# Attention's first pair and third load put in another order, and the first weight sums of the last expert layer ahead of the last mixes of the chunk before it

## The chip, the cores and the metric

The kernel runs on one NeuronCore of a Trainium2 chip. The metric is the device time of one execution in microseconds (us). Beside it stands the span of a profiled execution, from its first to its last instruction. TensorE (PE in the profile, PEld its weight loads) multiplies and transposes, VectorE (DVE), ScalarE (ACT) and GpSimd (POOL) work elementwise, and SyncE (SP) issues most of the transfers.

## The reference

Two parts, in float32. Part one is attention with rotary embedding for 2 batches of 8 heads, 576 tokens and head size 64; its output, 1152 tokens by 512, goes into part two, a dense mixture of 4 experts.

```
q_rot, k_rot = rotate(q), rotate(k)          # [x1*cos - x2*sin, x1*sin + x2*cos]
scores = scale * q_rot @ k_rot^T
attn = exp(scores - max) / sum
x = (attn @ v), heads side by side           # 1152 x 512
p = probs / sum(probs)
out = sum over e of p[:, e] * (relu(x @ w1[e]) @ w2[e])   # 512 -> 1024 -> 512
```

## The kernel before

Every float32 operand of a product is split into a high part in fp32r and a low part (value minus high part), and a product is the sum of three fp32r matmuls. ScalarE makes a high part (`wh`, `sh`, `hH`), GpSimd or VectorE the low one (`wl`, `sl`, `hL`).

**Attention** takes the heads in pairs: pairs 0 to 3 of batch 0 (list `first`), which run alone, and four of batch 1 (list `second`), which run beside the experts of chunk 0. A pair loads `rawk`, `rawq`, `rawv` (`Pair.load`), rotates k and q (`Pair.rotate`: two products into `t1` and `t2`, a sum, a split into `hlk` and `hlq`), transposes them on TensorE into a PSUM tile (`tpk`, `tpq`, the last 64 tokens `tlk`, `tlq`, `tlkq`) and copies that out with ScalarE (`kT`, `qT`). `k2T` is `kT` with its halves swapped, made by two transfers of `Pair.swap`. Then nine units u follow: scores `sc`, maximum `mx` on VectorE, exponential `e` on ScalarE, transposes `pp` and `x` of it, split `ptH`, `ptL`, `ptX`, and values. Pair 0 is rotated in pieces: tokens of head 0 and the tails first (columns 0 to NS), head 1 (columns NS to NC, four tiles of 64, 256 elements a partition) after. The score tiles and the `tpk`, `tpq` of a head share two PSUM buffers (tag `s`), used in turn. Pairs 0, 2 use the buffers `evens`, pairs 1, 3 `odds`, so pair 2's load writes the buffers from which pair 0 was rotated.

The order is written out by hand: `Agenda.at(t, f)` puts a step at a time t in units, and `run` calls the steps in the order of t; the times are tables (`FIRST_TURNS`, `TURNS`, `ALONE`). An engine executes what it was given in that order. A step of `load_qk(t, pr)` loads k and q of a pair and queues its rotation on GpSimd, of which `work` issues a piece every half unit.

**Experts.** Chunk 0 is 512 tokens, chunk 1 is 640. `Weights` loads w1 and w2 in blocks of 512 KB (`wr`, named chunk, expert, matrix, block) into `NRAW` = 2 raw buffers, and splits them into `wh` and `wl` (rings of 5). A raw block's buffer comes free when its last reader is done, which is GpSimd's `wl`, or VectorE for a block that is only summed. For chunk 0, `Moe.expert` makes the hidden layer and then four outputs `po`, which `mix` adds into `acc` on VectorE and, for the last expert, stores.

**The seam** is the passage from chunk 0 to chunk 1. For chunk 1 the first layer runs as seven products of half size in place of eight (`Moe1.product`, p1 to p7). They need sums of weight blocks (`Weights.sum`: four VectorE operations into `sf`, then `sh`, `sl`) and sums of x (`Quarters`). For expert 0 of chunk 1, blocks of w1 are loaded twice, once for `wh`, `wl` (matrix 0) and once for the sums (matrix 2), and then w2 (matrix 1). The first layer computes p1 and p2 of all four blocks (i = 0 to 3), then for each block p6, p7, p5, p4, p3. Each product goes to the next of eight PSUM banks (`Moe1.bank`), ScalarE copies p1 out, VectorE adds (`p`, `u`, `v`), ScalarE makes `hH` and VectorE `hL`. The second layer's `po` take the next five banks.

Of the kernel before, what the change touches and what calls it, by code (L numbers as in the profile page):

```python
# [49 lines left out]
]  # L50
FIRST_TURNS = dict(q0=(1.327, 1.797), q1=(1.739, 1.84), q_tails=(-0.037, 0.16), swap=0.18)
NEXT_TURNS = dict(tails=(-0.01, -0.008), k=(0.03, 0.056), q=(0.975, 1.004))
# [3 lines left out]
def kernel(  # L56
# [402 lines left out]
    class Weights:  # L459
# [14 lines left out]
        def load(self):  # L474
            if self.loaded == len(self.order):
                return
            key = self.order[self.loaded]
            c, e, which, fb = key
            lo, hi = fb * FB * P, (fb + 1) * FB * P
            src, f = (w2[e, lo:hi, :], DM) if which == 1 else (w1[e, :, lo:hi], FB * P)  # L480
            raw = wpool.tile([P, FB * DM], F32, tag="raw", name="wr%d_%d_%d_%d" % key, bufs=NRAW)
            nc.sync.dma_start(
                out=raw.rearrange("p (a f) -> p a f", f=f), in_=src.rearrange("(a p) f -> p a f", p=P)
            )
            self.raw[key] = raw, f
            self.loaded += 1
# [33 lines left out]
        def next(self):  # L520
            self.load()
            self.split()

    class Moe:
# [3 lines left out]
        def __init__(self, ctx, c, n_ps, lead):  # L528
            self.c = c
            self.lead, self.ph = lead, {}  # L530
            self.n = ctok[c]
# [11 lines left out]
        def expert(self, e):  # L543
# [24 lines left out]
            for f in range(NF):  # L568
                fb, fi = divmod(f, FB)
                wH, wL = (w[:, fi, :] for w in wts.got[c, e, 1, fb])  # L570
                for t in range(n // P):
# [4 lines left out]
                    if f == NF - 1:  # L576
                        self.mix(e, t, po[t])
                if e == E - 1 and f == NF - 2:
# [115 lines left out]
    class Moe1(Moe):  # L694
# [7 lines left out]
        def __init__(self, ctx, quarters):  # L702
# [6 lines left out]
            ]  # L709
            self.used = 0  # L710
            self.x, self.lows = {}, []

        def bank(self, name):
            x = self.pp.tile([P, 512], F32, tag=f"m{self.used % 8}", name=name)
            self.used += 1
            return x

# [56 lines left out]
        def first_layer(self, e):  # L774
# [3 lines left out]
            if e == 0:  # L778
                wts.split()
                wts.next()  # L780
                for p in ("p1", "p2"):
                    for i in range(nb):
                        self.product(e, i, p)
                wts.next()
            for i in range(nb):
                for p in ("p6", "p7", "p5", "p4", "p3") if e == 0 else ("p1", "p6", "p7", "p5", "p2", "p4", "p3"):
                    self.product(e, i, p)
                    if p == "p4":
                        wts.next()
                if e == 0 and i < 2:  # L790
                    wts.next()
# [147 lines left out]
    pr.keep_tails("k", True)  # L939
    pr.split_v(nc.scalar)  # L940
    nx.rotate_now("k", nc.gpsimd)
    nx.rotate_now("q", nc.gpsimd)
    nx.split_v()
    pr.rotate_now("k", nc.vector, NS, NC)
    rest = pr.rotate("q", nc.vector, NS, NC)
    for _ in range(3):
        next(rest)
    plan.at(1.5, lambda: next(rest))
    pr.turn_heads("k", (1,))
    pr.keep_heads("k", (1,))  # L950
    turn(FIRST_TURNS["q0"], pr, "q", (0,), False, (2, NR))
# [20 lines left out]
    for hp, pr in enumerate(first):  # L972
# [3 lines left out]
        if hp + 1 < NP:  # L976
# [7 lines left out]
            plan.at(n + t["swap"], nx.swap)  # L984
    load_qk(7.2, first[2])
    load_v(U + 5.8, first[2])
# [11 lines left out]
    chunk0 = ExitStack()  # L998
    tpool, quarters = [], []

# [4 lines left out]
    def start_experts():  # L1005
        spare.close()
        tpool.append(ctx.enter_context(tc.tile_pool(name="tpool", bufs=1)))
        moe = Moe(chunk0, 0, 4, 0).steps()
        for i in range(E * 2 * NF):
# [42 lines left out]
    plan.run()  # L1052
    chunk0.close()
    attn.close()


    with ExitStack() as chunk1:
        moe = Moe1(chunk1, quarters[0])
        wts.pool = moe.h
        for e in range(E):  # L1060
            moe.expert(e)
# [43 lines left out]
```

## Time and profile before

| what | value |
|---|---|
| median of 3 runs | 588.01 us (587.08 to 590.39) |
| the profiled execution | 588.56 us |
| its span | 586.8 us |
| TensorE busy | 548.2 us (93% of the span) |
| VectorE, ScalarE, GpSimd busy | 341.3, 279.4, 331.0 us |
| the chain that ended last | TensorE 73%, VectorE 11%, ScalarE 6%, GpSimd 5%, transfers 2%, issue 2% |
| mean granted TensorE clock | 0.990 |

TensorE's busy time is the largest, and the difference to the span, 38.6 us, is where it stood idle. The chain that ended last is followed back from the last instruction to whatever released each step; where it leaves TensorE, another engine or a transfer decided. The granted clock is the share of full speed that TensorE was given in a stretch: 1.00 is 2.4 GHz, 0.50 is 1.2 GHz. All times below count from the start of the span.

### The profile page before, as it was taken

Reading aid. Unit: us, or ns where it says so; the run is one execution under the profiler, and the core shown is the slowest. Engines: PE = TensorE matmul, PEld = TensorE weight load, DVE = VectorE, ACT = ScalarE, POOL = GpSimd, SP = SyncE. Lnnn points to the kernel's source line nnn. Section 1 sums busy time; section 2 is a strip of 40 time slices with the busy share of each in tenths; the row PEclk is TensorE's granted clock in tenths of the full one; section 3 lists DMA queues with packets and bytes.
Section 4 is the critical chain, followed back from the end, with each engine's and each line's share of the span. In section 5 each row is a group of like instructions: output and inputs, shape, how many; then the busy total and the mean of one; then the engine's idle time right before and its main releaser. Section 6 shows DMA issues by size and latency. Waiting matters only on the chain.

```text
span 586.8 us, 8596 instructions
## 1 busy us (share of the span) xinstructions
PE 548.2 (93%) x3229; PEld 480.3 (82%) x3229; DVE 341.3 (58%) x596; ACT 279.4 (48%) x545; POOL 331.0 (56%) x222
## 2 busy tenths in 40 slices
PE   3788888899999999999999998898999999999996
PEld 2677778788888888888888886896899889889985
DVE  6786889524353443444334435777678677767702
ACT  4685797456443555455436553444244335323400
POOL 6949991366933694279335386366663683465300
PEclk9998999899999999999999999899999999999999
DMA  5053232055125312532232222433233124223002
GB/s 152 18 158 78 63 99 60 0 150 175 45 73 156 92 37 72 135 113 73 72 100 77 67 73 71 144 110 106 74 107 108 47 81 126 68 74 104 8 0 89
DMA packets 42459, 50.67 MB, mean 86 GB/s; under 512 B 7218, under 2 KB 32050, under 8 KB 42418
## 3 DMA queue, kind: packets, MB, share of 16 engines
q1 hardware_dynamic: 41618, 49.38, 28.5%
q10 hardware_dynamic: 800, 0.75, 0.5%
q8 instruction: 25, 0.41, 0.3%
q14 instruction: 16, 0.13, 0.1%
HBM read 43.34 MB, written 2.36 MB: 78 GB/s over the span
## 4 chain that ended last, share of the span: by engine, by line
PE 73%; DVE 11%; ACT 6%; POOL 5%; DMA 2%; issue 2%; SPq 0%; ACTq 0%; DVEq 0%; POOLq 0%
PE po L808 6%; PE po L809 6%; PE po L810 6%; PE p L729 5%; PE p L730 5%; PE p L731 5%; PE sc L282 4%; PE ph L596 4%; PE ph L598 4%; PE ph L597 4%; PE po L575 4%; PE po L573 4%; PE po L574 4%; PE pp L315 3%; PE x L417 2%; ACT e L301 2%
## 5 line engine op out<-in xcount | busy, mean ns | idle before, releaser
L142 POOL TENSOR_TENSOR wl<-wr,wh 128x1024 fp32r<-128x1024 f32 x64 | 155.2, 2427 | 131.3 <-ACT wh L135 131.3
L135 ACT ACTIVATE wh<-wr 128x1024 fp32r<-128x1024 f32 x64 | 67.4, 1053 | 39.6 <-PE po L575 16.6
L293 DVE TENSOR_REDUCE mx<-sc 128x1 f32<-128x576 f32 x72 | 54.0, 752 | 35.8 <-PE sc L282 35.2
L142 POOL TENSOR_TENSOR sl<-sf,sh 128x1024 fp32r<-128x1024 f32 x16 | 38.6, 2417 | 50.2 <-ACT sh L135 46.2
L301 ACT ACTIVATE e<-sc,mx 128x576 f32<-128x576 f32 x72 | 53.3, 740 | 27.4 <-DVE mx L293 26.8
L808 PE MATMUL po<-wh,hH 128*128 128x512 f32 x160 | 62.6, 391 | 2.6 <-DVE hL L769 2.6
L809 PE MATMUL po<-wl,hH 128*128 128x512 f32 x160 | 62.3, 389 | 0.0
L810 PE MATMUL po<-wh,hL 128*128 128x512 f32 x160 | 62.3, 389 | 0.0
L559 DVE SCALAR_TENSOR_TENSOR hL<-ph,hH 128x512 fp32r<-128x512 f32 x32 | 22.1, 691 | 61.0 <-ACT hH L558 61.0
L315 PE MATMUL pp<-ident,e 128*128 128x128 f32 x288 | 45.7, 283 | 7.2 <-DVE e L387 4.2
L573 PE MATMUL po<-wh,hH 128*128 128x512 f32 x128 | 52.3, 409 | 0.0
L596 PE MATMUL ph<-xH,wh 128*128 128x512 f32 x128 | 51.5, 402 | 0.0
L332 ACT ACTIVATE ptH<-pp 128x512 fp32r<-128x512 f32 x64 | 38.1, 595 | 25.6 <-PE x L365 17.2
L575 PE MATMUL po<-wh,hL 128*128 128x512 f32 x128 | 50.2, 392 | 0.0
L598 PE MATMUL ph<-xH,wl 128*128 128x512 f32 x128 | 50.1, 392 | 0.0
L574 PE MATMUL po<-wl,hH 128*128 128x512 f32 x128 | 50.0, 391 | 0.0
L597 PE MATMUL ph<-xL,wh 128*128 128x512 f32 x128 | 50.0, 391 | 0.0
L336 DVE TENSOR_TENSOR ptL<-pp,ptH 128x512 fp32r<-128x512 f32 x64 | 43.8, 685 | 10.1 <-ACT ptH L332 9.6
L513 DVE TENSOR_TENSOR sf<-wr 128x256 f32<-128x256 f32 x32 | 39.3, 1268 | 15.5 <-DMA wr<-in_moe_w_dram 15.4
L767 ACT ACTIVATE hH<-p 128x320 fp32r<-128x320 f32 x64 | 27.4, 434 | 43.3 <-DVE p L759 43.0
L315 PEld LDWEIGHTS pp<-ident,e 128*128 128x128 f32 x288 | 34.6, 144 | 14.2 <-issue 4.1
L135 ACT ACTIVATE sh<-sf 128x1024 fp32r<-128x1024 f32 x16 | 17.0, 1060 | 59.1 <-DVE sf L513 59.1
(163 smaller groups left out, 1380.6 us busy)
## 6 DMA issues: line engine op xcount, KB each, us to landing
wr<-in_moe_w_dram SPq DMA_DIRECT2D x68, 512.0 KB, 3.6
k2T<-kT SPq DMA_DIRECT2D x14, 288.0 KB, 4.1
rawv<-in_v_dram SPq DMA_DIRECT2D x8, 256.0 KB, 2.8
out_dram<-acc SPq DMA_DIRECT2D x8, 256.0 KB, 2.5
rawk<-in_k_dram SPq DMA_DIRECT2D x7, 256.0 KB, 4.2
rawq<-in_q_dram SPq DMA_DIRECT2D x7, 256.0 KB, 3.2
rawv<-in_v_dram SPq DMA_DIRECT2D x16, 32.0 KB, 2.5
tabs<-in_rope_dram ACTq DMA_DIRECT2D x1, 320.0 KB, 3.4
```

Of the source, the lines that this page charges most:

```text
L135: nc.scalar.activation(out=hi, in_=src, func=AF.Copy)
L142: eng_l.tensor_tensor(out=lo, in0=src, in1=f32(hi), op=ALU.subtract)
L315: nc.tensor.transpose(pp[:, c * P : (c + 1) * P], self.e[u][:, c * P : (c + 1) * P], ident)
L573: nc.tensor.matmul(po[t], lhsT=sH, rhs=wH, start=(f == 0), stop=False)
L574: nc.tensor.matmul(po[t], lhsT=sH, rhs=wL, start=False, stop=False)
L575: nc.tensor.matmul(po[t], lhsT=sL, rhs=wH, start=False, stop=(f == NF - 1))
L596: nc.tensor.matmul(o, lhsT=wH[:, kt], rhs=xh, start=(kt == 0), stop=False)
L597: nc.tensor.matmul(o, lhsT=wH[:, kt], rhs=xl, start=False, stop=False)
L598: nc.tensor.matmul(o, lhsT=wL[:, kt], rhs=xh, start=False, stop=(kt == KT1 - 1))
L808: nc.tensor.matmul(po[t], lhsT=sH, rhs=wH, start=(f == 0), stop=False)
L809: nc.tensor.matmul(po[t], lhsT=sH, rhs=wL, start=False, stop=False)
L810: nc.tensor.matmul(po[t], lhsT=sL, rhs=wH, start=False, stop=(f == NF - 1))
```

## The change

Three edits.

1. **First pair.** The rotation of q of head 1 goes from VectorE to GpSimd, ahead of the rotations of pair 1. The transposes of k of head 1 leave the shared score buffers for the bank `xb[1]` and move behind the scores of unit 1; the copies of q move (`FIRST_TURNS`), and the swap of head 1 to unit 1.4.
2. **Third load.** k and q of pair 2 (`first[2]`) are loaded at unit 2.6 instead of 7.2.
3. **Seam.** The four mixes of chunk 0's last expert are kept back (`mixes`); ahead of them stand two loads and the sums of block 0, behind them a load and the sums of block 1. p1 goes to banks m4 to m7 and p2 to m0 to m3. Blocks 2 and 3 of matrix 2 get raw buffers of their own in a pool `sums`. The splits in `first_layer` of expert 0 move on by about half a block.

```diff
-FIRST_TURNS = dict(q0=(1.327, 1.797), q1=(1.739, 1.84), q_tails=(-0.037, 0.16), swap=0.18)
+FIRST_TURNS = dict(q0=(1.327, 1.45), q1=(2.3, 2.5), q_tails=(-0.037, 0.16), swap=1.4)
...
-            raw = wpool.tile([P, FB * DM], F32, tag="raw", name="wr%d_%d_%d_%d" % key, bufs=NRAW)
+            late = which == 2 and fb >= NRAW
+            raw = (self.pool if late else wpool).tile(
+                [P, FB * DM], F32, tag="raw", name="wr%d_%d_%d_%d" % key, bufs=NRAW
+            )
...
-                        self.mix(e, t, po[t])
+                        self.mixes.append((e, t, po[t]))
+                        if e < E - 1:
+                            self.mix(*self.mixes.pop())
...
-            self.used = 0
+            self.used, self.ahead = 4, [self.bank(f"p2_{i}", i) for i in range(4)]
...
-        def bank(self, name):
-            x = self.pp.tile([P, 512], F32, tag=f"m{self.used % 8}", name=name)
-            self.used += 1
-            return x
+        def bank(self, name, i=None):
+
+            if i is None:
+                i, self.used = self.used, self.used + 1
+                if 8 <= i < 12:
+                    return self.ahead[i - 8]
+            return self.pp.tile([P, 512], F32, tag=f"m{i % 8}", name=name)
...
-                wts.split()
-                wts.next()
                 for p in ("p1", "p2"):
                     for i in range(nb):
                         self.product(e, i, p)
-                wts.next()
+                wts.split()
             for i in range(nb):
...
-                    if p == "p4":
+                    if p == "p4" and (e or i):
                         wts.next()
-                if e == 0 and i < 2:
+                if e == 0 and i == 0:
+                    wts.split()
+                elif e == 0 and i in (1, 2):
                     wts.next()
...
+    pr.rotate_now("q", nc.gpsimd, NS, NC, odds)
     nx.rotate_now("k", nc.gpsimd)
...
-    rest = pr.rotate("q", nc.vector, NS, NC)
-    for _ in range(3):
-        next(rest)
-    plan.at(1.5, lambda: next(rest))
-    pr.turn_heads("k", (1,))
-    pr.keep_heads("k", (1,))
+    plan.at(1.1, lambda pr=pr: pr.turn_heads("k", (1,), tp=xb[1].bitcast(F32R).unsqueeze(1)))
+    plan.at(1.3, lambda pr=pr: pr.keep_heads("k", (1,)))
...
-    load_qk(7.2, first[2])
+    load_qk(2.6, first[2])
...
+        wts.pool = chunk1.enter_context(tc.tile_pool(name="sums", bufs=1, side="right", reuse_waits="tile"))
+        wts.load()
+        wts.load()
+        wts.split()
+        for x in moe0[0].mixes:
+            moe0[0].mix(*x)
+        chunk0.close()
+        wts.load()
+        wts.split()
         moe = Moe1(chunk1, quarters[0])
-        wts.pool = moe.h
```

What this makes of the order of instructions is shown at three places. The first is TensorE in pair 0, from the scores of unit 0 on; before:

```order
L231 MATMUL tpk_0_238<-identr,hlk_00_149 128x128 x4
L282 MATMUL sc_0_0_245<-kT_0_185,qT_0_188 128x288 x2
L282 MATMUL sc_0_0_245<-k2T_0_197,qT_0_188 128x288 x2
L254 MATMUL tlq_00_250<-identr,hlq_00_158 128x128
L282 MATMUL sc_0_1_259<-kT_0_185,qT_0_188 128x288 x2
L282 MATMUL sc_0_1_259<-k2T_0_197,qT_0_188 128x288 x2
L231 MATMUL tpq_0_266<-identr,hlq_00_158 128x128 x2
L315 MATMUL pp_0_0_269<-ident,e_0_0_257 128x128 x4
L231 MATMUL tpq_0_281<-identr,hlq_00_158 128x128 x4
L282 MATMUL sc_0_2_287<-kT_0_185,qT_0_188 128x288 x2
```

After the change (`x_113` is the bank `xb[1]`):

```order
L282 MATMUL sc_0_0_241<-kT_0_185,qT_0_188 128x288 x2
L282 MATMUL sc_0_0_241<-k2T_0_197,qT_0_188 128x288 x2
L254 MATMUL tlq_00_246<-identr,hlq_00_158 128x128
L282 MATMUL sc_0_1_253<-kT_0_185,qT_0_188 128x288 x2
L282 MATMUL sc_0_1_253<-k2T_0_197,qT_0_188 128x288 x2
L231 MATMUL x_113<-identr,hlk_00_149 128x128 x4
L231 MATMUL tpq_0_265<-identr,hlq_00_158 128x128 x2
L315 MATMUL pp_0_0_268<-ident,e_0_0_251 128x128 x4
L282 MATMUL sc_0_2_281<-kT_0_185,qT_0_188 128x288 x2
L282 MATMUL sc_0_2_281<-k2T_0_197,qT_0_188 128x288 x2
L341 MATMUL x_112<-ident,e_0_0_251 64x128
L231 MATMUL tpq_0_291<-identr,hlq_00_158 128x128 x4
```

The four transposes of k of head 1 went from ahead of unit 0's scores to behind unit 1's, and those of q of head 1 from ahead of unit 2's scores to behind them.

The second is VectorE at the seam, from the first of the four mixes (`acc`) or of the sums (`sf`) on; before:

```order
L606 SCALAR_TENSOR_TENSOR acc_0_1511<-po_3_0_3673,probs,acc_0_1511 128x512
L606 SCALAR_TENSOR_TENSOR acc_1_1512<-po_3_1_3674,probs,acc_1_1512 128x512
L606 SCALAR_TENSOR_TENSOR acc_2_1513<-po_3_2_3675,probs,acc_2_1513 128x512
L606 SCALAR_TENSOR_TENSOR acc_3_1514<-po_3_3_3676,probs,acc_3_1514 128x512
L513 TENSOR_TENSOR sf_0_3979<-wr_0_2_0_3886 128x256 x2
L513 TENSOR_TENSOR sf_0_3979<-sf_0_3979,wr_0_2_0_3886 128x256
L513 TENSOR_TENSOR sf_0_3979<-wr_0_2_0_3886,sf_0_3979 128x256
L513 TENSOR_TENSOR sf_1_3990<-wr_0_2_1_3920 128x256 x2
```

After the change:

```order
L516 TENSOR_TENSOR sf_0_3964<-wr_0_2_0_3885 128x256 x2
L516 TENSOR_TENSOR sf_0_3964<-sf_0_3964,wr_0_2_0_3885 128x256
L516 TENSOR_TENSOR sf_0_3964<-wr_0_2_0_3885,sf_0_3964 128x256
L611 SCALAR_TENSOR_TENSOR acc_0_1510<-po_3_0_3672,probs,acc_0_1510 128x512
L611 SCALAR_TENSOR_TENSOR acc_1_1511<-po_3_1_3673,probs,acc_1_1511 128x512
L611 SCALAR_TENSOR_TENSOR acc_2_1512<-po_3_2_3674,probs,acc_2_1512 128x512
L611 SCALAR_TENSOR_TENSOR acc_3_1513<-po_3_3_3675,probs,acc_3_1513 128x512
L516 TENSOR_TENSOR sf_1_3985<-wr_0_2_1_3919 128x256 x2
```

The sums of block 0 went ahead of the mixes; those of block 1 stayed behind them.

The third is ScalarE in chunk 1's first layer, from the high part of the third sums (`sh_2`) on; before:

```order
L135 ACTIVATE sh_2_4089<-sf_2_4084 128x1024
L767 ACTIVATE hH_0_1_4120<-p_0_4112 128x320
L767 ACTIVATE hH_0_1_4120<-p_0_4124 128x320
L135 ACTIVATE sh_3_4141<-sf_3_4136 128x1024
L767 ACTIVATE hH_0_0_4042<-p_0_4145 128x320
L135 ACTIVATE wh_0_1_0_4157<-wr_0_1_0_4134 128x1024
L767 ACTIVATE hH_0_3_4188<-p_1_4180 128x320
L767 ACTIVATE hH_0_3_4188<-p_1_4192 128x320
L135 ACTIVATE wh_0_1_1_4204<-wr_0_1_1_4155 128x1024
```

After the change:

```order
L135 ACTIVATE sh_2_4093<-sf_2_4088 128x1024
L775 ACTIVATE hH_0_1_4124<-p_0_4116 128x320
L775 ACTIVATE hH_0_1_4124<-p_0_4128 128x320
L775 ACTIVATE hH_0_0_4051<-p_0_4138 128x320
L135 ACTIVATE sh_3_4153<-sf_3_4148 128x1024
L775 ACTIVATE hH_0_3_4184<-p_1_4176 128x320
L775 ACTIVATE hH_0_3_4184<-p_1_4188 128x320
L135 ACTIVATE wh_0_1_0_4200<-wr_0_1_0_3983 128x1024
L775 ACTIVATE hH_0_2_4061<-p_1_4204 128x320
L135 ACTIVATE wh_0_1_1_4216<-wr_0_1_1_4198 128x1024
```

`sh_3` moved behind the third `hH` of block 0, and `wh_0_1_0`, the first high part of w2, behind the two `hH_0_3` of block 1; each later split of w2 moved by as much.

## Rows read from the trace of the kernel before

**Rows 1.** Timeline, VectorE, first pair: start, length, engine, line, output<-inputs, shapes, count [idle before]
```profile
11.25 0.42 DVE L142 TENSOR_TENSOR hlk<-t1k,hlk 128x256 fp32r<-128x256 f32 x1
...
12.05 1.84 DVE L189 TENSOR_TENSOR t2q<-rawq,tabs 128x128 f32<-128x128 f32 x2
...
15.36 1.41 DVE L293 TENSOR_REDUCE mx<-sc 128x1 f32<-128x576 f32 x2
```

**Rows 2.** Timeline, ScalarE and TensorE, first pair
```profile
16.14 0.74 ACT L301 ACTIVATE e<-sc,mx 128x576 f32<-128x576 f32 x1 [2.09 <-DVE mx L293]
...
17.02 0.50 PE L231 MATMUL tpq<-identr,hlq 128*128 128x128 f32 x2 [2.23 <-ACT e L301]
...
24.40 0.30 PE L341 MATMUL x<-ident,e 128*64 128x128 f32 x1 [0.82 <-DVE ptX L348]
```

**Rows 3.** Timeline, GpSimd, first pair and start of the second
```profile
7.39 0.72 POOL L185 TENSOR_TENSOR t1q<-rawq,tabs 128x192 f32<-128x192 f32 x1
...
10.43 0.64 POOL L142 TENSOR_TENSOR hlq<-t1q,hlq 128x192 fp32r<-128x192 f32 x1
...
13.70 1.45 POOL L185 TENSOR_TENSOR t1k<-rawk,tabs 128x576 f32<-128x576 f32 x1
```

**Rows 4.** Timeline, GpSimd, rotation of pair 2
```profile
37.97 1.41 POOL L185 TENSOR_TENSOR t1k<-rawk,tabs 128x576 f32<-128x576 f32 x1 [8.23 <-DVE ptL L336]
...
43.44 1.40 POOL L142 TENSOR_TENSOR hlk<-t1k,hlk 128x576 fp32r<-128x576 f32 x1
...
50.15 1.42 POOL L142 TENSOR_TENSOR hlq<-t1q,hlq 128x576 fp32r<-128x576 f32 x1
```

**Rows 5.** Timeline, SyncE's queue, load of pair 2
```profile
31.44 1.28 SPq L162 DMA_DIRECT2D rawk<-in_k_dram  x1
```

**Rows 6.** Timeline, TensorE, transposes of pairs 1 and 2
```profile
33.30 0.51 PE L231 MATMUL tpq<-identr,hlq 128*128 128x128 f32 x4
...
44.90 0.53 PE L231 MATMUL tpk<-identr,hlk 128*128 128x128 f32 x4 [1.98 <-POOL hlk L142]
...
52.18 0.24 PE L254 MATMUL tlkq<-identr,hlq 128*128 128x128 f32 x1
```

**Rows 7.** Windows: stretch, length, busy us by engine, granted clock, DMA share, GB/s
```profile
46.00:48.00 2.00, 2.00 (x15) 1.70 (x15) 0.00 (x0) 0.23 (x2) 1.92 (x4) 0.55 0.03 8
48.00:50.00 2.00, 2.00 (x12) 1.93 (x11) 0.45 (x2) 1.09 (x2) 1.91 (x2) 0.60 0.48 137
```

**Rows 8.** Timeline, TensorE, the seam and start of the second layer
```profile
368.55 0.41 PE L729 MATMUL p<-xH,wh 128*128 128x320 f32 x1 [1.71 <-DVE acc L606]
...
370.53 0.64 PE L729 MATMUL p<-xH,wh 128*128 128x320 f32 x1 [0.83 <-DVE acc L606]
...
400.44 0.50 PE L808 MATMUL po<-wh,hH 128*128 128x512 f32 x1 [0.87 <-DVE hL L769]
```

**Rows 9.** Timeline, VectorE, the seam
```profile
367.76 2.72 DVE L606 SCALAR_TENSOR_TENSOR acc<-po,probs,acc 128x512 f32<-128x512 f32 x4
370.39 0.75 DVE L513 TENSOR_TENSOR sf<-wr 128x256 f32<-128x256 f32 x2
...
386.55 0.48 DVE L759 TENSOR_TENSOR u<-p,p 128x320 f32<-128x320 f32 x1
...
390.89 0.48 DVE L759 TENSOR_TENSOR u<-p,p 128x320 f32<-128x320 f32 x1
```

**Rows 10.** Timeline, VectorE, a later sum of weights
```profile
408.27 2.61 DVE L513 TENSOR_TENSOR sf<-wr 128x256 f32<-128x256 f32 x1
```

**Rows 11.** Timeline, GpSimd, the split before the second layer, and one beside rows 10
```profile
389.38 4.78 POOL L142 TENSOR_TENSOR wl<-wr,wh 128x1024 fp32r<-128x1024 f32 x2
...
408.02 2.57 POOL L142 TENSOR_TENSOR wl<-wr,wh 128x1024 fp32r<-128x1024 f32 x1
```

**Rows 12.** Timeline, ScalarE, the seam
```profile
374.45 1.40 ACT L736 ACTIVATE p<-p 128x320 f32<-128x320 f32 x4
...
395.85 1.06 ACT L135 ACTIVATE wh<-wr 128x1024 fp32r<-128x1024 f32 x1 [4.54 <-DMA wr<-in_moe_w_dram]
```

More of the change, by code (lines that the diff above doesn't have):

```diff
@@ L529, in __init__ @@
             self.c = c
-            self.lead, self.ph = lead, {}
+            self.lead, self.ph, self.mixes = lead, {}, []
             self.n = ctok[c]
@@ L998 @@
     chunk0 = ExitStack()
-    tpool, quarters = [], []
+    tpool, quarters, moe0 = [], [], []
     def narrow():
@@ L1007, in start_experts @@
         tpool.append(ctx.enter_context(tc.tile_pool(name="tpool", bufs=1)))
-        moe = Moe(chunk0, 0, 4, 0).steps()
+        moe0.append(Moe(chunk0, 0, 4, 0))
+        moe = moe0[0].steps()
         for i in range(E * 2 * NF):
@@ L1052 @@
     plan.run()
-    chunk0.close()
     attn.close()
     with ExitStack() as chunk1:
+        wts.pool = chunk1.enter_context(tc.tile_pool(name="sums", bufs=1, side="right", reuse_waits="tile"))
[7 more added lines that the diff above has]
+        wts.split()
         moe = Moe1(chunk1, quarters[0])
-        wts.pool = moe.h
         for e in range(E):
```

## The prediction

> **What bounds the kernel now.** TensorE is busy for 93% of the span, so a change pays only where TensorE stands idle or is slowed. I read TensorE's waits first, then the timelines of the engines that it waited for. Three places bear on the change.
>
> *First pair.* The maxima of units 0 and 1 start on VectorE only at 15.36, because the rotation of q's second head stands ahead of them; two of its products take 1.84 us there. The first exponential starts at 16.14, and TensorE, which waits 2.23 us for it, goes on at 17.02 [rows 1, 2].
>
> *Pair 2.* GpSimd stands idle for 8.23 us until 37.97, when pair 2's k and q begin to arrive; their load was issued at 31.44. The rotated k is ready at 44.84 (43.44 and 1.40). TensorE waits 1.98 us for it until 44.90 and then runs slowly: granted 0.55 and 0.60 of full speed in two windows of 2 us, which is 2 x 0.45 + 2 x 0.40 = 1.7 us lost [rows 4 to 7].
>
> *The seam.* TensorE waits 1.71 us for the first mix (368.55), works on one product, and waits 0.83 us more for the last mix (370.53). Later the second layer is held until 400.44 [rows 8]. The reader is to see that this second hold is not TensorE's own: 395.85 shows ScalarE waiting 4.54 us for a block of w2, with the hidden layer's copies queued behind, and that block could be loaded only when GpSimd's split of an earlier w2 block (389.38) had freed its raw buffer [rows 11, 12].
>
> **The change part by part.** Times are of the execution before; the sums are made against its own 588.56 us.
>
> *1. The maxima come sooner.* VectorE is now free at 11.67 (11.25 and 0.42), and four transposes leave the queue ahead of unit 0's scores. The scores end at about 12.7, the maximum (0.7) at 13.4, the first exponential (0.74) at 14.2, 2.7 earlier than before. Then gains are given back. ScalarE now copies k of head 1 (from about 14.7) and q's tiles ahead of the second exponential, which starts at about 15.8. Unit 2's scores take the buffer of unit 1, so they start at 16.6. Unit 3's take the buffer of unit 2, and ScalarE's exponential of unit 2 stands behind the copy of q's second head, which waits for GpSimd. GpSimd starts that rotation at about 13.7, where pair 1's began. Its length is not in the trace. From below: 256 of pair 2's 576 elements in 6.87 us (37.97 to 44.84) gives 3.1. From above: the rotation of 192 elements took 3.68 (7.39 to 11.07), times 256/192 is 4.9. I take 3.9, between them, since the small one ran beside VectorE's rotation. So it ends at 17.6, the copy at 19.4, the exponential of unit 2 at 20.1; the transpose `x` of unit 2 that stood at 24.40 comes at about 23.2 [rows 1 to 4]. **Gain 1.2** (bounds 0.2, with the rotation at 4.9, to 2.0, with the short one).
>
> By the Trainium skill (GPSIMD Engine Reference, Engine selection) elementwise work with two inputs belongs on VectorE, GpSimd being about half as fast. The rows agree on the ratio (0.42 for 256 elements at 11.25; 0.64 for 192 at 10.43), and by that rule alone the edit would cost time, about 590. It leaves out what the row at 12.05 shows: with both engines at work the operation took its 1.84 on VectorE too, and GpSimd had 8.23 us to spare.
>
> *2. GpSimd's queue.* Behind the rotation stand pair 1's k, q and v, all 3.9 us later. q of pair 1 then ends at about 31.4 and is wanted at 33.30 less 1.2, which just holds. v ends at 33.6, and there pair 2's rotation now follows, since its load stands behind pair 0's swap and is issued at about 16.5, 15 us ahead. SyncE has nothing else queued that is due before then. Pair 2's k is ready at 40.6 instead of 44.84 and is wanted at 44.90 - 1.98 - 1.2 = 41.7: the wait is gone, and with it the slow stretch. **Gain 1.98 + 1.7 = 3.7.** What is next to be late is q of pair 2: it ended at 51.57, now at 47.3, and is wanted at 52.18 - 1.2 - 3.7 = 47.3. So 4.9 is the most that both edits can give, and a later GpSimd lowers it one for one [rows 3 to 7].
>
> *3. VectorE beside a busy GpSimd.* Around 34 to 38 GpSimd now works where it was idle. A VectorE operation with inputs from SBUF alone can be held for the whole of a GpSimd instruction: 408.27 took 2.61, to the end of the split that began at 408.02, where two such sums took 0.75 at 370.39 [rows 9 to 11]. Pair 0's division of the last unit meets this. I charge **0.2**, since pair 1's exponentials have slack on ScalarE there (bounds 0 and 1.4, one rotation instruction).
>
> *4. The seam.* The sums of block 0 take 1.46 (370.39 to where 371.85 ends the same four) and start where the mixes did, at 367.8. Mixes: 369.3 to 372.0. TensorE starts p1 at once at 366.8 in banks that attention left, and is in p2's second product when the last mix ends: it wins here 3 us at first. But ScalarE has made block 0's high sums by 370.5, and GpSimd's low part (2.4, as at 389.38) runs to 372.95. By the row at 408.27 the sums of block 1, due at 372.0, wait for that, and end at 374.4; the high part takes ScalarE to 375.5, and only then come the copies of p1, which began at 374.45 before. So VectorE's additions start no sooner than they did, at about 376.0, and they take as long as TensorE's products: 4.34 us a block (386.55 to 390.89). The first w2 split stands behind two hidden copies of block 1. Counted in VectorE's steps, its low part starts at about 390.6 instead of 389.38, 1.25 later, and so does everything up to the load of the third w2 block, which ScalarE gets at 397.1 instead of 395.85. In its favour, the hidden copy that opens the second layer now stands behind the third block, not the fourth. High part 1.06, hidden copy and low part 0.9: TensorE goes on at 399.1 instead of 400.44, **gain 1.3**. It has then been idle for about 3.4 us (its products end at 394.3, two groups of the second layer at 395.7). After the 1.98 us at 44.90 the clock fell, so I take that it does here: **minus 1.7**, as priced above. The seam gives -0.4 (bounds: -1.7, the clock lost and no gain, to +2.4, the hold at 372.0 not paid and the clock kept) [rows 7 to 12]. The raw buffers of their own cost nothing: two loads more stand ahead of the mixes' stores, and no one waits for those stores until the second layer.
>
> **Sum.** 1.2 + 3.7 - 0.2 - 0.4 = 4.3. 588.56 - 4.3 = 584.3; the profiled execution is 0.55 above the median of 588.01, so the median comes to **583.7**.
>
> **The rivals.**
>
> *A, the seam pays.* If TensorE's clock holds through the wait at 396, the seam is +1.3; if moreover the sums of block 1 are not held, up to +2.4. For it: the waits of 1.71 at 368.55 and of 0.87 at 400.44 are shorter than the new one, so nothing shows what one ahead of long matmuls costs. Time: 583.7 - 1.7 = 582.0, at best 580.9.
>
> *B, GpSimd is late for pairs 1 and 2.* If the moved rotation takes 4.9 or more, q of pair 1 misses 32.1 and q of pair 2 misses 47.3, and the waits return: 1.0 in edit 1, and 1.0 to 1.5 at the pairs. Time about 586.0. For it: VectorE and GpSimd hold each other up. Against: VectorE has little from SBUF to do in that stretch now.
>
> *C, slower.* The mixes stand behind the sums of block 0, whose buffer lies where attention's data were. If these sums have to wait for the transfers into that memory, the two new 512 KB loads among them, all of the seam waits with them, TensorE at p2 first. They pass the point where everything is lost at 4.3 us late, and two loads one behind the other, at 4 us each as 391.8 to 395.85 shows for one, make about 8 less the 3.8 between 364 and 367.8: 4.2 to 5, and another slow stretch of 1.7. Time about 590. Against: the raw blocks have buffers of their own, so only old transfers should count.
>
> *D, the early load doesn't come early.* If q's load waits on the queue until GpSimd has read pair 0's q, it is still issued by 18; it would have to slip past 30 to matter. Time 587.
>
> **How the numbers follow.** The forecast (4.3, within 582.8 to 585.0) gets 0.45, A 0.27, B 0.18, C 0.05, D 0.05. Half a per cent, 2.9 us, is about what a measurement tells from no change: faster means below 585.1. The forecast counts 0.42 faster and 0.03 same; A all faster; B 0.03 faster, 0.14 same, 0.01 slower; C 0.01 same and 0.04 slower; D 0.01 faster, 0.03 same, 0.01 slower. Together faster 0.73, same 0.21, slower 0.06. The range of 8 in 10 takes in A but its best end, and most of B: 580.8 to 586.8.
>
> **What would show it.** Right: `mx` at 12.7, TensorE's `tpk` of pair 2 without a wait and a granted clock near 1.00 from 40 to 48; GpSimd without its idle 8 us; p1 at the seam straight behind `po`; the sums of block 1 held till `sl` ends; a wait of about 3 us before the second layer and a low clock behind it. Wrong: a wait for `hlq` of pair 1 or 2, a first `sf` that starts much after the last quarter step, or a second layer that opens before 398.

## The result, and the profile after

The changed kernel takes 581.70 us (median of 4 runs, 580.44 to 583.32) beside 587.55 for the kernel before (4 runs): a ratio of 0.9892, 95% interval 0.9848 to 0.9937, so about 1.1% faster. The profiled execution takes 582.67 with a span of 580.9; the one before took 588.56 with 586.8, so the two traces differ by 5.89. The forecast was 583.7, within 580.8 to 586.8.

To see where 5.89 us come from, I took the n-th exponential of ScalarE in both traces (there are 72, in the same order) and then the starts of TensorE's stages. "Ahead" is how much sooner the changed kernel gets there:

| marker | before | after | ahead |
|---|---|---|---|
| 1st exponential | 16.14 | 12.80 | 3.34 |
| 6th | 27.30 | 26.07 | 1.23 |
| 13th | 43.33 | 42.09 | 1.24 |
| 14th (behind the transposes of pair 2's k) | 50.62 | 45.78 | 4.84 |
| 16th | 56.77 | 51.09 | 5.68 |
| 19th | 64.56 | 59.11 | 5.45 |
| 31st | 93.48 | 89.03 | 4.45 |
| 37th | 131.47 | 126.03 | 5.44 |
| last product of chunk 0 begins | 361.12 | 355.75 | 5.37 |
| second layer of chunk 1 begins | 397.81 | 388.72 | 9.09 |
| expert 1 of chunk 1 begins | 426.40 | 420.41 | 5.99 |
| last product | 581.75 | 575.87 | 5.88 |

Between these two executions, what edits 1 and 2 touch gives 5.4 (up to the last product of chunk 0) and the seam 0.5; the experiments show how far that holds for others. The timeline after, first pair and pair 2 (columns as in [rows 1]):

```profile
12.01 0.76 DVE L293 TENSOR_REDUCE mx<-sc 128x1 f32<-128x576 f32 x1 [0.27 <-PE sc L282]
...
12.80 0.74 ACT L301 ACTIVATE e<-sc,mx 128x576 f32<-128x576 f32 x1 [0.41 <-DVE mx L293]
...
13.45 0.73 POOL L185 TENSOR_TENSOR t1q<-rawq,tabs 128x256 f32<-128x256 f32 x1
...
15.54 0.53 SPq L162 DMA_DIRECT2D rawk<-in_k_dram  x1
...
16.39 0.72 POOL L142 TENSOR_TENSOR hlq<-t1q,hlq 128x256 fp32r<-128x256 f32 x1
...
17.17 0.75 PE L231 MATMUL tpq<-identr,hlq 128*128 128x128 f32 x4 [0.96 <-POOL hlq L142]
...
38.43 1.64 POOL L142 TENSOR_TENSOR hlk<-t1k,hlk 128x576 fp32r<-128x576 f32 x1
...
41.54 0.51 PE L231 MATMUL tpk<-identr,hlk 128*128 128x128 f32 x4
...
47.36 0.25 PE L254 MATMUL tlkq<-identr,hlq 128*128 128x128 f32 x1
```

The maximum stands at 12.01 where [rows 1] had 15.36; GpSimd turns q's second head from 13.45 to 17.11. Pair 2's load is issued at 15.54, not 31.44 [rows 5]; its rotated k is ready at 40.07 (38.43 and 1.64) and TensorE takes it at 41.54 with no wait, where [rows 6] show 1.98. Its q, ready at 46.85, is taken at 47.36.

The seam after, same columns:

```profile
361.30 0.30 PE L737 MATMUL p<-xH,wh 128*128 128x320 f32 x1
...
365.11 2.39 POOL L142 TENSOR_TENSOR sl<-sf,sh 128x1024 fp32r<-128x1024 f32 x1 [7.03 <-ACT sh L135]
...
366.49 1.63 DVE L516 TENSOR_TENSOR sf<-wr 128x256 f32<-128x256 f32 x2
...
366.62 0.42 PE L737 MATMUL p<-xH,wh 128*128 128x320 f32 x1 [0.76 <-DVE acc L611]
...
370.43 0.42 PE L737 MATMUL p<-tH,sh 128*128 128x320 f32 x1 [0.90 <-ACT p L744]
...
391.13 1.06 ACT L135 ACTIVATE wh<-wr 128x1024 fp32r<-128x1024 f32 x1 [3.27 <-DMA wr<-in_moe_w_dram]
392.09 0.42 ACT L775 ACTIVATE hH<-p 128x320 fp32r<-128x320 f32 x1
...
393.09 0.79 PE L816 MATMUL po<-wh,hH 128*128 128x512 f32 x1 [2.81 <-DVE hL L777]
...
421.21 3.38 DVE L609 TENSOR_SCALAR acc<-po,probs 128x512 f32<-128x512 f32 x5
```

TensorE starts p1 at 361.30 with no wait, against 1.71 in [rows 8]. The pair of sums at 366.49 takes 1.63 instead of the 0.75 of [rows 9]: it ends after the split that GpSimd began at 365.11. The long wait has moved to the second layer (2.81). The row at 391.13 says why: ScalarE waits 3.27 for a block of w2, and the hidden copy at 392.09 stands behind it in its queue.

The granted clock (third figure from the end) in windows of the kernel after, then of the kernel before:

```profile
17.00:24.00 7.00, 6.30 (x28) 5.62 (x29) 3.55 (x6) 3.93 (x9) 6.59 (x8) 0.51 0.30 84
...
392.00:396.00 4.00, 2.91 (x7) 2.33 (x8) 2.68 (x6) 2.22 (x5) 3.54 (x2) 0.57 0.29 98
```

```profile
17.00:24.00 7.00, 6.21 (x32) 5.50 (x32) 4.36 (x6) 4.31 (x10) 6.67 (x7) 1.00 0.01 0
46.00:50.00 4.00, 4.00 (x25) 3.63 (x25) 0.45 (x2) 1.31 (x3) 3.83 (x5) 0.57 0.25 73
107.00:111.00 4.00, 3.48 (x15) 2.96 (x16) 2.34 (x6) 0.60 (x1) 0.00 (x0) 0.58 0.00 0
370.00:374.00 4.00, 3.47 (x13) 3.48 (x14) 3.33 (x9) 1.57 (x2) 0.90 (x1) 0.57 0.78 260
```

Up to TensorE's last product these are all the stretches with a low granted clock; the window 17 to 24 of the kernel before stands there for comparison. Before: three that lose 1.7 us each, by the estimate 4.00 x 0.43 = 1.7. After: one of 3.4 (7.00 x 0.49) and one of 1.7. So by this column both traces lose about 5.1 to the clock, and it doesn't explain the 5.89. Two things limit that reading. The kernel before, too, ran at the lower level up to about 22, under a granted clock of 1.00 (last section). And a loss counts only if nothing holds TensorE later: after the stretch at 370 to 374 it waits 1.76 for `hL` at 397.81 all the same.

### The profile page after: what moved, and what is told of

Read it like the earlier page. It is cut to its first block, busy times and chain, and to the rows that moved or that the text cites. A ratio compares the mean times of both kernels' runs of the same rounds, so it can differ in the third digit from the quotient of the medians.

```text
span 580.9 us, 8599 instructions
## 1 busy us (share of the span) xinstructions
PE 545.8 (94%) x3229; PEld 477.9 (82%) x3229; DVE 335.1 (58%) x590; ACT 279.1 (48%) x545; POOL 334.7 (58%) x228
## 4 chain that ended last, share of the span: by engine, by line
PE 73%; DVE 9%; ACT 8%; POOL 4%; DMA 3%; issue 2%; SPq 0%; ACTq 0%; POOLq 0%; DVEq 0%
PE po L816 6%; PE po L818 6%; PE po L817 6%; PE sc L282 5%; PE ph L601 4%; PE ph L603 4%; PE ph L602 4%; PE p L737 4%; PE p L738 4%; PE p L739 4%; PE po L578 4%; PE po L576 4%; PE po L577 4%; PE pp L315 4%; ACT e L301 3%
```

## The experiments

Theory: edits 1 and 2 carry the gain by the two places named in the prediction, and the seam gives next to nothing because something behind it is late. Rivals: the gain is one wait counted in two edits; or the seam is worth 2 us and hides it behind a slow clock. Each time is set against the kernel before in the same session, with the 95% interval of the ratio.

**One edit at a time.** The kernel before with edit 1 (first pair), with edit 2, with the seam, and with edits 1 and 2:

```diff
-    load_qk(7.2, first[2])
+    load_qk(2.6, first[2])
```

(this line is the whole of edit 2; edit 1 is the hunks of `FIRST_TURNS` and of the first pair, the seam is all the others.)

> The kernel before with edit 1 alone (first pair reordered). Theory: the maxima of units 0 and 1 come about 3 us sooner, and about 1.2 us of it is left by the sixth exponential (27.30 before, 26.1 now); pair 2's load is still placed late, so GpSimd still stands idle before pair 2 and TensorE still waits about 2 us there, 1.2 us earlier than before. Time about 1.2 us less than before. Rival: the moved rotation makes GpSimd late and nothing is left at pair 2 (time as before, a wait at pair 2 longer by 1.2).

> The kernel before with edit 2 alone (the third load placed early). Theory: GpSimd's idle 8 us are gone and so are the wait of 1.98 us for the rotated k of pair 2 and the slow clock behind it: 3.6 us less than before at unit 13's exponential, with the time about 3.5 to 4.5 us less than before. Rival: without edit 1 the wait only moves to q of pair 1 or to a VectorE operation held by GpSimd, and less than 2 us are gained.

> The kernel before with edit 3 alone (the seam). Theory from the trace after: the seam as a whole is worth +0.5 us, no more: it saves the first mixes' wait, is 1.7 us ahead at the second layer, and loses most of it to a slow clock behind a wait of 2.8 us there. Time 0 to 1 us less than before. Rival (the predicted step): it costs 0.4 us. Second rival: the seam keeps its clock here and gains 2 to 2.5 us.

> The kernel before with edits 1 and 2. Theory: these two carry the whole gain: about 5.4 us less than before by the end of attention (the last division's exponentials at 344.5 instead of 349.85), time about 5.4 us less. Rival: edits 1 and 2 overlap, since both move the same wait, and together give no more than edit 2 alone.

| kernel | median | kernel before | ratio, interval |
|---|---|---|---|
| edit 1 alone | 585.06 | 587.01 | 0.9953 (0.9918 to 0.9989) |
| edit 2 alone | 583.06 | 587.01 | 0.9945 (0.9919 to 0.9971) |
| seam alone | 587.47 | 587.01 | 1.0004 (0.9981 to 1.0027) |
| edits 1 and 2 | 582.45 | 587.01 | 0.9931 (0.9897 to 0.9966) |

Edits 1 and 2 are each faster, together most of the change; the seam alone can't be told from nothing. That excludes the second rival for the seam (2 to 2.5 if the clock holds), and its trace says so more sharply. This execution had no low granted clock at the seam: 1.00 in each 4 us from 392 to 404. Expert 1 begins 63.25 after the last product of chunk 0 begins (360.73 to 423.98), where before it was 65.28 (361.12 to 426.40): 2.0 ahead. But expert 1's second layer begins at 450.21, which is 89.48 after that mark and 89.91 before: 0.4 is left. Of the 2.0, 1.6 were given back in expert 1's first layer, which took 26.23 instead of 24.63.

The other traces bear this out. From the beginning of chunk 0's last product to expert 1's second layer it takes 89.24 to 89.91 in the four traces with the seam as it was (before, edit 1, edit 2, edits 1 and 2), and 89.34 to 90.06 in the five with the new seam unaltered (the changed kernel twice, the seam alone, and two kernels of further below: ScalarE for the held operations, and filled waits). In three of these five the granted clock falls at about 392, in two it stays at 1.00 (89.48 and 90.06). So the 0.5 of the first table is within the scatter of executions, and the seam gives nothing with either clock.

Edits 1 and 2 together give 4.6 in medians (5.4 expected), alone 2.0 and 4.0; the intervals are too wide to say whether they overlap by a us, so that rival stays open to this extent. Single traces scatter too: with edits 1 and 2 (the fastest of its six runs was profiled) the 72nd exponential is 7.80 ahead of before, in the changed kernel, with the same code up to there, 5.36. Held operations and slow stretches, both below, fall differently in each execution. The trace of edit 1 alone shows one thing that was expected and one that was not: at the 13th exponential it is 1.7 ahead (41.60), and then pair 2's wait and a slow stretch of 3.4 from 44 to 51 leave 0.4 at the 15th.

**What holds the second layer.** Three changes of the changed kernel. In the first, three splits (w2's third and fourth block, expert 1's first) stand behind the first layer; in the second, p1 is copied ahead of block 1's sums; the third is both.

```diff
-                    if p == "p4" and (e or i):
+                    if p == "p4" and (e or i == 1):
                         wts.next()
...
-                elif e == 0 and i in (1, 2):
+                elif e == 0 and i == 1:
                     wts.next()
             for f in self.lows:
                 f()
             self.lows = []
+            if e == 0:
+                for _ in range(3):
+                    wts.next()
```

```diff
                     for i in range(nb):
                         self.product(e, i, p)
-                wts.split()
+                    wts.next() if p == "p1" else wts.split()
...
         chunk0.close()
-        wts.load()
-        wts.split()
         moe = Moe1(chunk1, quarters[0])
```

> The changed kernel once more, for the spread of its time and its slow stretches on the same chip as the variants. Theory: TensorE's slow stretches, 1.7 or 3.4 us of loss each, fall in the first pair and at the second layer in most executions, and their number makes the spread; median about 581.7, between 578 and 583.5. Rival: the spread has nothing to do with the granted clock.

> The changed kernel with the splits of the third and fourth w2 block and of expert 1's first block moved behind the first layer's last hidden copies. Theory: the hold of 2.81 us at the second layer is ScalarE's queue (a split that waits 3.27 us for its transfer stands ahead of the hidden copy); without it TensorE runs on at 388.7 without a wait and without the slow stretch of 1.7 behind it: about 4.5 us less than the changed kernel, some 577. Rival: VectorE's hidden low halves are late by themselves, and the wait stays over 1.5 us. Second rival: the third block, split later, is now late for the second layer's third quarter, and the wait moves there (no gain).

> The changed kernel with p1's products and copies ahead of block 1's sums. Theory: ScalarE copies p1 at once instead of behind the high part of block 1, the wait of 0.90 us (and the 0.76 stays) goes, and VectorE's chain up to the second layer comes about 1 us sooner: 0.9 us less than the changed kernel. Rival: the chain of block transfers decides when the second layer opens, and nothing is gained; block 1's low part, 1 us later on GpSimd, may even hold the second block's products.

> Both of these edits. Theory: they add, 5.4 us less than the changed kernel, some 576.3. Rival: the same as with the late w2 splits alone.

The changed kernel again: 581.16 (before 587.05; ratio 0.9902, 0.9870 to 0.9935). Splits behind: 580.95 (0.9909, 0.9879 to 0.9938). Copies first: 580.02 (0.9872, 0.9837 to 0.9907). Both: 581.15 (0.9908, 0.9881 to 0.9935). Nothing was gained by the first, against my theory of 4.5, and the second's 1.1 (0.9 expected) is inside the intervals. The repeated trace of the changed kernel has low granted clocks at 17 to 24, 102 to 106 and 392 to 396. TensorE's starts tell why:

| kernel | seam's p1 | second layer | expert 1 | first mix of expert 0 | p1 to mix |
|---|---|---|---|---|---|
| changed | 361.30 | 388.72 | 420.41 | 421.21 | 59.9 |
| splits behind | 360.33 | 387.75 | 414.98 | 420.13 | 59.8 |
| copies first | 360.52 | 386.62 | 418.34 | 418.85 | 58.3 |
| both | 360.52 | 386.61 | 413.84 | 420.16 | 59.6 |
| four raw buffers (below) | 361.81 | 387.89 | 415.12 | 412.60 | 50.8 |

With the splits behind, the second layer runs without a wait (27.23 from 387.75 to 414.98, as in later experts), so the theory of ScalarE's queue is right for that wait. But it moved one stage on: expert 1's products need the banks that the mixes free, and in all four kernels the mixes start 58.3 to 59.9 us after p1, whether the second layer waits or not. The kernel with both edits, VectorE and TensorE at expert 1:

```profile
415.45 4.00 DVE L516 TENSOR_TENSOR sf<-wr 128x256 f32<-128x256 f32 x2 [2.34 <-DMA wr<-in_moe_w_dram]
...
420.16 3.38 DVE L609 TENSOR_SCALAR acc<-po,probs 128x512 f32<-128x512 f32 x5
...
420.96 0.63 PE L737 MATMUL p<-t1H,sh 128*128 128x320 f32 x1 [4.32 <-DVE acc L609]
```

The mixes stand on VectorE behind the sums of expert 1's fourth block, and these wait for its transfer. In the changed kernel the sums of expert 1 wait at the same place:

```profile
402.48 3.59 DVE L516 TENSOR_TENSOR sf<-wr 128x256 f32<-128x256 f32 x2
...
409.36 3.96 DVE L516 TENSOR_TENSOR sf<-wr 128x256 f32<-128x256 f32 x2 [2.50 <-DMA wr<-in_moe_w_dram]
...
416.75 3.75 DVE L516 TENSOR_TENSOR sf<-wr 128x256 f32<-128x256 f32 x2 [2.64 <-DMA wr<-in_moe_w_dram]
```

One block each 7.1 us on average ((416.75 - 402.48) / 2): with two raw buffers a load can start only when GpSimd has split the block two before. Each of these pairs of sums also takes 3.6 to 4.0 instead of 0.75, and ends 0.3 after a split on GpSimd does (405.79, 413.04 and 420.21).

**More raw buffers.** The seam's own two raw buffers lie idle once chunk 1's first sums are made. Here they are used on, in turn with the old two, so that loads run four blocks ahead; p1's copies come first, and only expert 1's first block is split behind the first layer.

```diff
-            late = which == 2 and fb >= NRAW
+            late = c and (e or which) and fb >= NRAW
...
                     for i in range(nb):
                         self.product(e, i, p)
-                wts.split()
+                    wts.next()
...
-                    if p == "p4" and (e or i):
+                    if p == "p4" and (e or i in (1, 2)):
                         wts.next()
-                if e == 0 and i == 0:
-                    wts.split()
-                elif e == 0 and i in (1, 2):
+                if e == 0 and i < 3:
                     wts.next()
...
+            if e == 0:
+                wts.next()
...
-        wts.load()
-        wts.split()
         moe = Moe1(chunk1, quarters[0])
```

> p1's copies first, and four raw buffers in turn for all blocks of chunk one behind the first sums (the two of the pool of the sums are used on, so loads run four blocks ahead instead of two); the first block of expert 1 is split behind the first layer. Theory: what bounds the seam is the supply of blocks, some 7.2 us for each with two raw buffers, since a load waits until GpSimd has split the block two before; with four, neither the wait of 2.6 us at the second layer nor the one at expert 1 stays, and with them a slow stretch goes: 4 to 6 us less than the changed kernel, 575.5 to 577. Rival: GpSimd, at 5 us for each block with its sums, and VectorE's sums held by it are the bound, and the waits only shrink by half. Second rival: no gain at all, something else (the mixes) opens expert 1.

Measured: 576.20 (before 585.91; ratio 0.9812, 0.9766 to 0.9857). VectorE at the mixes, and TensorE's waits from 358 to 440 us (what waits, for whom, us in total, times, longest):

```profile
412.60 3.47 DVE L609 TENSOR_SCALAR acc<-po,probs 128x512 f32<-128x512 f32 x5 [4.34 <-PE po L818]
```

```profile
PE p L737 <- DVE acc L611: 0.8, 1, 0.8
PE p L737 <- DVE hL L777: 0.2, 1, 0.2
```

The mixes now wait for TensorE (4.34 for its last product), not the other way round; the second layer takes 27.23 and expert 1's first layer 24.63, both without a wait. Its trace has no low granted clock from 107 to the last product. The sums of expert 1's four blocks begin at 392.54, 394.82, 398.67 and 406.71, the last 10.0 sooner than in the changed kernel. They are still held (5.13 at 398.67), so the rival that VectorE's held sums are the bound is out. So the supply of blocks was what bounded the seam. Four buffers in the unaltered order were not run; but with two buffers, the copies first and the later splits gave nothing that could be told from no change.

**VectorE's held operations.** In the changed kernel the last unit's scaling and the spreading of the inverse sums go to ScalarE; 1e-9 is not added to the sums (this leaves out that one step of the reference).

```diff
-            nc.vector.tensor_scalar_add(self.total, self.total, 1e-9)
             nc.vector.reciprocal(out=self.total, in_=self.total)
...
-            nc.vector.tensor_scalar_mul(e, e, self.total[:, TAIL:])
+            nc.scalar.activation(out=e, in_=e, func=AF.Copy, scale=self.total[:, TAIL:])
...
-            nc.vector.tensor_copy(self.rep, by_row.unsqueeze(3).to_broadcast([P, NR, 2, D]))
+            nc.scalar.activation(out=self.rep, in_=by_row.unsqueeze(3).to_broadcast([P, NR, 2, D]), func=AF.Copy)
```

> The changed kernel with the last unit's scaling and the spreading of the inverse sums on ScalarE instead of VectorE, and without adding 1e-9 to sums that are at least 1; VectorE keeps the reciprocal. Theory: VectorE's operations on data in SBUF were held by GpSimd's instructions (0.17 to 2.3 us for the same operation), and TensorE waited for them 1.10, 1.15 and 1.92 us in pairs 2 and 3; the reciprocal, 0.22 in every row, is not held. These three waits shrink by 2 us or more in sum, and the time by 2 to 3.5. Rival: ScalarE, busy for over 80% of these stretches, is late in its turn and TensorE waits for it as long as before; no change.

Measured: 577.56 (before 585.91; ratio 0.9841, 0.9802 to 0.9879). That is 8.4 less than the kernel before, where the changed kernel was 5.9 less; the two intervals overlap a little, so the 2.5 between them is likely, not certain. In place of the wait of 1.10 stand one of 0.81, for ScalarE's copy of q, and one of 0.37; that of 1.15 is gone; that of 1.92 is 0.62, for ScalarE, with 1.00 behind it. In sum 4.17 became 2.80. What leaving out the addition gives by itself was not measured. TensorE's rows of this kernel:

```profile
99.18 0.66 PE L315 MATMUL pp<-ident,e 128*128 128x128 f32 x4 [0.62 <-ACT e L386]
100.84 0.30 PE L341 MATMUL x<-ident,e 128*64 128x128 f32 x1 [1.00 <-DVE ptX L348]
```

At the 37th exponential it is 8.07 ahead of the kernel before, where the changed kernel is 5.44. No low granted clock follows here, but one does in the last kernel below, with the same edit.

**The first pair's waits filled.** TensorE repeats transposes of units 0 and 1 in its waits (the results are written twice, the same).

```diff
-            for c in range(NR):
+            for c in list(range(NR)) * (2 if self is first[0] and u < 2 else 1):
...
-            nc.tensor.transpose(px[:, i * P : (i + 1) * P], self.e.pop(u)[:, SM:S], ident)
+            for _ in range(8 if self is first[0] and u == 0 else 1):
+                nc.tensor.transpose(px[:, i * P : (i + 1) * P], self.e[u][:, SM:S], ident)
+            self.e.pop(u)
```

> The changed kernel with transposes of the first pair done again in TensorE's waits (four each of units 0 and 1, seven of the short one of unit 0). Theory: TensorE's clock falls at 17 because of its waits of 0.78, 0.96 and 0.54 us just before; with them filled it stays at 1.00 there, no execution has a slow stretch in the first pair, and the time is 0.6 to 1.6 us less, with less spread. Rival: the clock falls all the same, or the first pair is bound by GpSimd and ScalarE anyway, and the time stays within 0.5.

Measured: 578.60 (577.25 to 582.16; before 585.91; ratio 0.9877, 0.9830 to 0.9925). The granted clock stays at 1.00 from 8 to 24 in its trace, but so it does in three traces without filling (edit 1 alone, copies first, both). The transposes tell more: the four at about 20 us take 0.60 here and in the kernel with all three edits below, and 1.06 in all nine other traces with edit 1. (Of the waits that the expectation names, the one of 0.54 ended at 19.32, after the clock had fallen.) At the 6th exponential these two are 2.61 and 2.88 ahead, the nine 0.68 to 2.18. In the time the step can't be told from the changed kernel's, whose interval overlaps.

**All three together** (four raw buffers, ScalarE for the held operations, filled waits):

> Four raw buffers, no VectorE operation of the last unit for GpSimd to hold, and the filled waits of the first pair, all in the changed kernel. Theory: the three act at different places and add: 5 us at the seam (two waits and a slow stretch), 3.5 in pairs 2 and 3 and the last pair, 1 to 1.5 in the first pair: 571 to 573 us, and a smaller spread. Rival: they overlap (a clock kept in one place falls in another), and the time is 574 to 575.5.

Measured: 570.40 (569.83 to 571.26, 6 runs; before 586.88; ratio 0.9727, 0.9704 to 0.9750), so 16.5 less than the kernel before, where the changed kernel was 5.9 less. The 10.6 between them put the time just below the range that I gave for adding gains. Reckoned in the same way the three alone gave 3.8, 2.5 and 1.4, in sum 7.7: they don't overlap, and why the three together give more stays open. Of slow stretches its trace has one up to the last product, 1.7 us at 99 to 104. The runs now lie within 1.4 us of one another.

## Why the prediction was right, point by point

**Maxima sooner: 1.2 forecast, 1.24 measured**, so close by luck. The first exponential came 3.34 sooner, not 2.7, and the rotation took 3.66 (13.45 to 17.11), not 3.9. I had not put in that TensorE would work slowly from 17 to 24 (granted 0.51; four transposes took 1.06). The kernel before was slow there too, but only up to about 22: its four transposes took 1.06 at 20.55 and 0.60 at 22.45. In the filled kernel 2.61 were kept. So two errors met; the nine traces without filling have 0.68 to 2.18 at the 6th exponential, all but one within my bounds of 0.2 to 2.0.

**Pair 2: 3.7 forecast, 3.60 measured** (1.24 to 4.84). Ready at 40.07 (forecast 40.6), no wait, granted clock 1.00 from 25 on. The limit of 4.9 set by q of pair 2 was not reached: q was ready at 46.85 and taken at 47.36. Nor is it firm: in the trace of edits 1 and 2 alone q was ready at 46.73, and the 14th exponential is 5.26 ahead.

**VectorE held by GpSimd: -0.2 forecast, -0.38 measured**, not at the place that I had charged. Pair 0's division lost nothing (1.24 ahead at the 7th and at the 13th exponential). The short operations on the experts' shares `probs`, beside pair 1, were held before and free after (+0.84, 14th to 16th exponential); all eleven traces with edit 2 gain 0.6 to 0.85 there. The last unit's operations of pair 1 and of pair 2 were held longer (-0.23 and -0.99); these two differ from execution to execution. So the sum came near by luck. VectorE before, then VectorE, GpSimd and TensorE after:

```profile
53.70 0.79 DVE L126 TENSOR_SCALAR ptot<-ptot 128x9 f32<-128x9 f32 x1
54.53 0.22 DVE L127 RECIPROCAL ptot<-ptot 128x9 f32<-128x9 f32 x1
54.78 1.23 DVE L128 TENSOR_TENSOR probs<-probs,ptot 128x36 f32<-128x36 f32 x1
...
83.56 1.08 DVE L382 TENSOR_SCALAR total<-total 128x9 f32<-128x9 f32 x1
```

```profile
48.86 0.17 DVE L126 TENSOR_SCALAR ptot<-ptot 128x9 f32<-128x9 f32 x1
49.07 0.22 DVE L127 RECIPROCAL ptot<-ptot 128x9 f32<-128x9 f32 x1
49.32 0.48 DVE L128 TENSOR_TENSOR probs<-probs,ptot 128x36 f32<-128x36 f32 x1
...
77.77 2.39 POOL L142 TENSOR_TENSOR wl<-wr,wh 128x1024 fp32r<-128x1024 f32 x1
78.12 2.08 DVE L382 TENSOR_SCALAR total<-total 128x9 f32<-128x9 f32 x1
...
81.23 0.66 PE L315 MATMUL pp<-ident,e 128*128 128x128 f32 x4 [1.10 <-DVE e L387]
```

The same operation on the same shape takes 0.17 or 2.08, here to the end of GpSimd's split (77.77 and 2.39 make 80.16), and the last row is the wait that TensorE gets from it.

**Not in the sum: +0.99.** Before, a slow stretch stood at 107 to 111, behind a wait of 1.92. After, the same wait is there, with 1.00 behind it. No step of the change speaks of it.

**The seam: -0.4 forecast, +0.51 measured.** Its steps came in the order forecast. Less the 5.37 gained ahead of it: the sums of block 1 end at 368.90 (forecast 374.4 - 5.37 = 369.0), the copies of p1 start at 369.96 (370.1), w2's first low part at 384.82 (385.2), the third block comes to ScalarE at 391.13 (391.7), and the second layer goes on at 393.09 (393.7). That opening is 1.98 ahead of [rows 8], where I had 1.3, and the slow stretch of 1.7 behind it came. Counted from the beginning of chunk 0's last product, the opening stands at 38.6 to 39.3 in the four traces with the old seam and at 37.2 to 37.6 in the five with the new, so 1.3 was a fair price. What failed is the step from the opening to the time. Neither the 1.3 gained nor the 1.7 lost is left at expert 1's second layer, which comes 89.2 to 89.9 after that point with the old seam and 89.3 to 90.1 with the new, whether the clock held or fell. **Rival A and the upper bound of 2.4** fail by the same step: a clock that holds does not pay, because the blocks of expert 1 come no sooner. My view ended at the opening of the second layer; that the two terms came to -0.4, near nothing, is luck. Under A I also wrote that the shorter waits show nothing of the cost of one ahead of long matmuls. Behind those of 1.71 and 0.83 the granted clock was 0.57 from 370 to 374, in the trace that I had.

B did not come (the rotation was short), nor C (the sums of block 0 start at 362.38, on time), nor D (issued at 15.54). Sum: 1.24 + 3.60 - 0.38 + 0.99 - 0.08 (small drift to the end of attention) + 0.51 = 5.88 against 4.3. Of the 1.58 between them the slow stretch at 107, which nothing foretold, is 0.99 and the seam 0.91; the other terms take 0.32 off. As seen, both of the large ones are chance, of the two executions that were profiled. The median nevertheless fell by 5.9 twice: seven traces with edits 1 and 2 and otherwise unaltered attention begin the last product of chunk 0 4.9 to 7.8 sooner than the kernel before (6.0 in the mean), where the first three terms made 4.7. The steady part of what they lacked is the 0.6 to 0.85 at `probs`.

## What to carry to other kernels

A wait taken from TensorE's queue moves to the next thing that is late: before pricing it, follow the supply (load, split, buffer free again) to the next stage that needs it, and compare its rate with the stage's. Here a wait of 2.8 us could be removed without any gain, until loads ran four blocks ahead. When a queue holds an operation that waits for a transfer, whatever is queued behind it is late too; and buffers that a short stage got for itself may serve the long one after it.

## What the runs showed of the hardware that I had not expected

**The spread goes with the granted clock, in part.** Ten runs of edit 1 alone lie from 579.91 to 586.81 us; the four at a mean granted clock of 0.996 to 0.997 take 579.9 to 580.8, the six at 0.985 to 0.991 take 584.9 to 586.8. It is not all: three runs of the changed kernel at the same 0.994 lie 2.2 us apart (579.30 to 581.46). And the same wait of 1.92 us in front of the same transposes was followed by 0.58 in one execution (before, 107 to 111) and by 1.00 in another (after, 103.07). A single profile can't price a wait's clock.

**A granted clock of 1.00 in this column doesn't mean that TensorE runs at full speed.** Edit 1 alone shows 1.00 from 17 to 24, and in that stretch four transposes take as long as in the slow stretch of the changed kernel. Windows and TensorE rows of edit 1 alone, then TensorE rows of the filled kernel:

```profile
17.00:24.00 7.00, 6.47 (x32) 5.76 (x31) 3.79 (x7) 4.45 (x11) 6.67 (x7) 1.00 0.01 0
```

```profile
20.15 1.06 PE L315 MATMUL pp<-ident,e 128*128 128x128 f32 x4
...
25.51 0.63 PE L315 MATMUL pp<-ident,e 128*128 128x128 f32 x4
```

```profile
19.84 0.60 PE L315 MATMUL pp<-ident,e 128*128 128x128 f32 x4
```

The same work takes 1.06, and 0.63 or 0.60: the length of a known instruction tells the two levels (1.2 and 2.4 GHz) apart, where the column did not. The Trainium skill (TensorE: Matmul & The Clock Gate, "What's actually happening") says that the low level is the state at the start and that work releases it; these rows agree, slow first and fast later. It also says that records of the clock have been seen to be unreliable ("Seeing it yourself"); the first fence looks like such a case.

**The reciprocal was never held.** It takes 0.21 or 0.22 in all 126 rows of the 14 traces, 59 of them with GpSimd at work, while the addition ahead of it (L382) takes 0.17 to 2.08 and the scaling behind it (L387) 0.51 to 2.33. The product of `probs` with two inputs (L128) took 1.23 or 0.48 above, and the copy `rep` 0.41 to 2.34. The Trainium skill (SBUF — State Buffer, "Who interferes with whom") says that VectorE's `tensor_scalar` and `copy` can hold a pair of ports in common with GpSimd, that two inputs from SBUF do too, and that other operations with one input from SBUF don't; the rows agree with each part, the last for the reciprocal alone.
